# v of batch 0 in three pieces of 4, 2 and 2 heads, and a feed-forward unit moved ahead of the fourth tile, in an attention plus GEGLU kernel

## The chip, the cores and the metric

The kernel runs on one core of a Trainium2 chip. The metric is device time in microseconds (us), as the median of several executions. Executions of this kernel agree within about 0.3%. The span of a profile is up to 1.9 us shorter than the device time of the same execution, so spans are compared with spans and times with times.

Names: PE is the matmul engine, PEld its weight loads, DVE is VectorE, ACT is ScalarE, POOL is GpSimd, SP is SyncE. PSUM, the matmul results' memory, is used here as eight banks.

## The reference, cut to what matters

```python
q, k, v: (8 batches, 8 heads, 576 rows, 64)            # float32
q_p = [relu(q)*cos, relu(q)*sin];  k_p likewise          # by position
kv  = k_p^T v ;  z = sum of k_p over rows                # per batch and head
x   = (q_p kv) / (q_p z + 1e-6)  -> (4608 tokens, 512)
out = (gelu(x @ w_gate) * (x @ w_val)) @ w_out           # 512 -> 1536 -> 512
```

## The kernel before

The 576 rows of a batch are four tiles of 128 and one of 64. Tile t of batch 0 goes through these steps: scale q (`sq`), turn it (`q_by_pe`, copied out of PSUM by ScalarE or VectorE), multiply it by kv (`numer_mm`), divide (`norm`, VectorE), and turn x (`x_by_pe`, `X`). The columns of the feed-forward part that x then allows are done in units: a `gate` (four matmuls, then a Gelu on ScalarE) and a `value` (four matmuls, then a product on VectorE). `A` stands for the 256 columns of the first two tiles. `dummies(n)` are filler matmuls, whose results nobody reads. A transfer of k or v comes as two, one for the odd and one for the even partitions, and a tile needs both.

```python
def gate(n, jt, c0, w, gb):            # gb: PSUM bank
    for ct in range(CT): nc.tensor.matmul(ps[:, gb, 0:w], ...)
    nc.scalar.activation(gel[:, 0:w], ps[:, gb, 0:w], AF.Gelu)
def value(n, jt, c0, w, vb):
    for ct in range(CT): nc.tensor.matmul(ps[:, vb, 0:w], ...)
    nc.vector.tensor_mul(hT..., gel[:, 0:w], ps[:, vb, 0:w])
def gv_unit(n, jt, c0, w, gb, vb, mid=()):      # gate, mid, value
...
def Y(t, bank): ...      # numerator of tile t into banks bank and bank+1, then norm
def X(t, bank, eng): ... # turn x of tile t
...
q_by_pe(0, 3, 6, "s")                  # tile 3, copied by ScalarE
gate(0, 2, *A, 5)
X(2, 0, "v")()
sq(4, 1, "s"), sq(4, 0, "v")           # scale q of the last tile
gate(0, 3, *A, 4)
value(0, 2, *A, 7)
Y(3, 0)()
value(0, 3, *A, 2)
q_by_pe(0, 4, 3, "s")
gv_unit(0, 0, 256, 128, 5, 6)
gv_unit(0, 1, 256, 128, 4, 7, (X(3, 0, "s"),))
Y(4, 2)()
...
# k and v of batch 1: issued when the first piece of w_out has landed
nc.gpsimd.tensor_copy(kf[0:2, 0, 0, 0:1], wo_sb[0:2, 2, C - 1:C])
load_k(1)
```

Each engine is given its work in the order of the text. The tiles are counted from 0: tile 3 is the fourth. The recorded texts sometimes say "the third tile" for it.

Of the kernel before, what the change touches and what calls it, by code (L numbers as in the profile page):

```python
# [16 lines left out]
def kernel(  # L17
# [44 lines left out]
    vf = sb.tile([128, H, NJ + 1, D], FP32, name="vf")  # L62
# [13 lines left out]
    def load(dst, t, b, h0=0, h1=H, even=None, odd=None, j0=0, j1=NJ + 1):  # L76
        runs = t[b, h0:h1].rearrange("h (i r) d -> i h r d", r=9)
        for s, r0, n, eng in ((1, 5, 4, odd), (0, 0, 5, even)):
            n = min(n, j1)
            (eng or nc.sync).dma_start(  # L80
                out=dst[s:128:2, h0:h1, j0:n].rearrange("p h j d -> p h (j d)"),
                in_=runs[:, :, r0 + j0:r0 + n].rearrange("i h r d -> i h (r d)"),
            )
# [14 lines left out]
    nc.gpsimd.memset(vf[:, :, NJ], 0.0)  # L98
    load(qf, q, 0, j1=2)
    load(vf, v, 0, 0, 4)  # L100
    load(vf, v, 0, 4, 8)
    load(qf, q, 0, j0=2)

    nc.vector.tensor_scalar(par_i, par_i, 1, None, op0=ALU.bitwise_and)  # L104
# [20 lines left out]
    def dummies(n, bank=7):  # L125
        for _ in range(n):
            nc.tensor.matmul(ps[:, bank, :], lhsT=junk[:, 0:128], rhs=junk, start=True, stop=True)  # L127


    def scale(f, j, which, eng, h0=0, h1=H):  # L130
        dst, src = f
        col = (cos_c if which == 0 else sin_c)[:, j:j + 1]
        s, d = src[:, h0:h1, j, :], dst[:, j, h0:h1, which * D:(which + 1) * D]
        if eng == "v":
            nc.vector.tensor_scalar(d, s, col, 0.0, op0=ALU.mult, op1=ALU.max)  # L135
        else:
            nc.scalar.activation(d, s, AF.Relu, scale=col)  # L137

    def cast_v(b, h0, h1, eng="v"):
        cp = nc.vector.tensor_copy if eng == "v" else nc.scalar.copy  # L140
        cp(vx[b % 2][:, :, h0:h1, 0:D], vf[:, h0:h1].rearrange("p h j d -> p j h d"))  # L141
# [6 lines left out]
        )  # L148


    def kv_half(b, g, bank, eng="s"):
        for h in range(4 * g, 4 * g + 4):
            for j in range(NJ + 1):
                nc.tensor.matmul(  # L154
                    ps[:, bank, (h % 4) * (D + 1):(h % 4 + 1) * (D + 1)],
                    lhsT=kp[:, j, h, :],
                    rhs=vx[b % 2][:, j, h, 0:D + 1],
                    start=(j == 0), stop=(j == NJ),
                )
        if eng is not None:  # L160
            kv_evac(b, g, bank, eng)

    def kv_evac(b, g, bank, eng):
        src = ps[:, bank, 0:4 * (D + 1)].rearrange("p (h e) -> p h e", e=D + 1)
        dst = kv[b % 2][:, 4 * g:4 * g + 4, 0:D + 1]
        (nc.scalar.copy if eng == "s" else nc.vector.tensor_copy)(dst, src)
# [10 lines left out]
    def norm(xb, bank, g0, g1, rows=128):  # L177

        n = g1 - g0
        nd = ps[0:rows, bank + g0:bank + g1, 0:4 * (D + 1)].rearrange("p g (h e) -> p g h e", e=D + 1)  # L180
        den = rot.tile([128, 2, 4], FP32, name="den")
        nc.vector.tensor_scalar(den[0:rows, 0:n], nd[:, :, :, D], EPS, None, op0=ALU.add)  # L182
        rec = rot.tile([128, 2, 4], FP32, name="rec")
        nc.vector.reciprocal(rec[0:rows, 0:n], den[0:rows, 0:n])  # L184
        nc.vector.tensor_tensor(  # L185
            xb[0:rows, g0:g1], nd[:, :, :, 0:D],
            rec[0:rows, 0:n, :, None].to_broadcast([rows, n, 4, D]), op=ALU.mult,
        )

    def new_xb():  # L190
        return rot.tile([128, 2, 4, D], BF16, name="xb", bufs=4)
# [22 lines left out]
    def gate(n, jt, c0, w, gb):  # L214

        p0 = starts[n] + c0
        for ct in range(CT):
            nc.tensor.matmul(  # L218
                ps[:, gb, 0:w], lhsT=wg_sb[:, ct, jt * 128:(jt + 1) * 128],
                rhs=xT[:, ct, p0:p0 + w], start=(ct == 0), stop=(ct == CT - 1),  # L220
            )
        gels[n, jt, c0] = gel = rot.tile([128, 512], FP32, name="gel", bufs=4)
        nc.scalar.activation(gel[:, 0:w], ps[:, gb, 0:w], AF.Gelu)  # L223

    def value(n, jt, c0, w, vb):

        p0 = starts[n] + c0
        for ct in range(CT):
            nc.tensor.matmul(  # L229
                ps[:, vb, 0:w], lhsT=wv_sb[:, ct, jt * 128:(jt + 1) * 128],  # L230
                rhs=xT[:, ct, p0:p0 + w], start=(ct == 0), stop=(ct == CT - 1),
            )
        gel = gels.pop((n, jt, c0))
        nc.vector.tensor_mul(hT[n % 2][:, jt, 64 + c0:64 + c0 + w], gel[:, 0:w], ps[:, vb, 0:w])  # L234

    def gv_unit(n, jt, c0, w, gb, vb, mid=()):
        gate(n, jt, c0, w, gb)
        for f in mid:
            f()
        value(n, jt, c0, w, vb)  # L240
# [63 lines left out]
    def load_w(j0, j1):  # L304
        nc.gpsimd.dma_start(out=wg_sb[:, :, j0 * 128:j1 * 128], in_=wg_r[:, :, j0 * 128:j1 * 128])
        nc.gpsimd.dma_start(out=wv_sb[:, :, j0 * 128:j1 * 128], in_=wv_r[:, :, j0 * 128:j1 * 128])
# [13 lines left out]
    def q_by_pe(b, j, bank, eng, h0=0, h1=H):  # L320

        qb = ps[:, bank, :].bitcast(BF16).rearrange("p (h t) -> p h t", h=H)
        for h in range(h0, h1):
            nc.tensor.transpose(out=qb[:, h, :], in_=qp[:, j, h, :], identity=ident)  # L324
        if eng is not None:
            q_evac(b, j, bank, eng, h0, h1)

    def q_evac(b, j, bank, eng, h0=0, h1=H):
        qb = ps[:, bank, :].bitcast(BF16).rearrange("p (h t) -> p h t", h=H)
        cp = nc.vector.tensor_copy if eng == "v" else nc.scalar.copy  # L330
        if j < NJ:
            cp(qT[b % 2][:, j, h0:h1], qb[:, h0:h1])
        else:
            cp(qT[b % 2][:, j, h0:h1, 0:64], qb[:, h0:h1, 0:128:2])

    def x_by_pe(b, t, xb, bank, eng, c0=0, c1=CT):
        p0 = b * S + t * 128
        cp = nc.vector.tensor_copy if eng == "v" else nc.scalar.copy
        xb2 = xb.rearrange("p g h d -> p (g h d)")
        rows = 128 if t < NJ else 64  # L340
        view = ps[:, bank, 0:256].bitcast(BF16).rearrange("p (c t) -> p c t", c=CT)
        for ct in range(c0, c1):
            nc.tensor.transpose(  # L343
                out=view[:, ct, 0:rows], in_=xb2[0:rows, ct * 128:(ct + 1) * 128], identity=ident[0:rows, 0:rows],
            )
        cp(xT[:, c0:c1, p0:p0 + rows], view[:, c0:c1, 0:rows])  # L346

    def sq(j, which, eng, *h):
        scale(Q, j, which, eng, *h)
# [11 lines left out]
    load_w(0, 2)  # L361
    load_w(2, 4)
    load_w(4, 8)
    for j in range(2):
        sq(j, 0, "v"), sq(j, 1, "s")
        q_by_pe(0, j, j, None)
    dummies(3)
    q_evac(0, 0, 0, "v")
    cast_v(0, 0, 2, "v")
    cast_v(0, 2, 4, "s")  # L370
    kv_half(0, 0, 4, None)
    q_evac(0, 1, 1, "v")
    dummies(2)
    cast_v(0, 4, 6, "v")
    cast_v(0, 6, 8, "s")
    kv_evac(0, 0, 4, "v")
    kv_half(0, 1, 5, "s")
    x0, x1 = new_xb(), new_xb()
    numer_mm(0, 0, 6, 0)
    norm(x0, 6, 0, 1)  # L380
    dummies(1, 4)
    numer_mm(0, 0, 6, 1)
    sq(2, 1, "s")
    norm(x0, 6, 1, 2)
    sq(2, 0, "v")
    numer_mm(0, 1, 0, 0)
    numer_mm(0, 1, 0, 1)
    norm(x1, 0, 0, 2)
    x_by_pe(0, 0, x0, 4, "s", 0, 2)
    dummies(2, 5)  # L390
    x_by_pe(0, 0, x0, 4, "s", 2, 4)
    q_by_pe(0, 2, 3, None)

    nc.gpsimd.tensor_copy(tiny[0:1, 1:2], x0[0:1, 1, 3, D - 1:D])
    load_w(8, 12)
# [2 lines left out]
    A, Bw = (0, 256), (256, 320)  # L398
    xs = {1: x1}

    def X(t, bank, eng):
        return lambda: x_by_pe(0, t, xs[t], bank, eng)

    def Y(t, bank):
        def f():
            xs[t] = numer(0, t, bank, 128 if t < NJ else 64)
        return f

    gate(0, 0, 0, 128, 5)
    gate(0, 1, 0, 128, 4)  # L410
    X(1, 2, "s")()
    q_evac(0, 2, 3, "v")
    sq(3, 0, "v"), sq(3, 1, "s")
# [5 lines left out]
    value(0, 0, 128, 128, 2)  # L419
    value(0, 1, 128, 128, 3)  # L420
    q_by_pe(0, 3, 6, "s")
    gate(0, 2, *A, 5)
    X(2, 0, "v")()
    sq(4, 1, "s"), sq(4, 0, "v")
    gate(0, 3, *A, 4)
    value(0, 2, *A, 7)
    Y(3, 0)()
    value(0, 3, *A, 2)
    q_by_pe(0, 4, 3, "s")
    gv_unit(0, 0, 256, 128, 5, 6)  # L430
    gv_unit(0, 1, 256, 128, 4, 7, (X(3, 0, "s"),))
    Y(4, 2)()
    gv_unit(0, 0, 384, 128, 5, 1)
    gv_unit(0, 1, 384, 128, 4, 0)
    gate(0, 4, *A, 5)
    X(4, 7, "v")()
    gate(0, 5, *A, 4)
    gv_unit(0, 2, *Bw, 2, 6)
    gv_unit(0, 3, *Bw, 3, 7)
    value(0, 4, *A, 1)  # L440
    value(0, 5, *A, 2)
    gv_unit(0, 0, 512, 64, 4, 6)
    gv_unit(0, 1, 512, 64, 5, 7)


    load_q(1, nc.gpsimd)
# [24 lines left out]
    for jt in range(4, 12):  # L471
        for i, (c0, w) in enumerate((A, Bw)):
            if (jt, i) not in ((4, 0), (5, 0)):
                j = 0 if jt == 4 else i
# [57 lines left out]
    for n in range(1, 7):  # L532
        b = n + 1
# [5 lines left out]
        s = 0 if n > 1 else -1  # L539
# [70 lines left out]
```

## Time and profile before

| | before |
|---|---|
| device time, median | 326.25 us (325.94 to 326.5, 4 runs; 326.3 over the first 3) |
| span of the profile | 324.7 us |
| PE busy | 317.4 us (98%) |
| PE idle between 20 and 26 us | 0.08 us |
| product of batch 1's k and v begins | 48.68 us |

The page and chain of waits of this kernel are in the prediction below. PE has almost nothing left to give, so a change of the first 30 us shows as the lateness or earliness with which PE leaves that stretch.

### The profile page before, as it was taken

Reading aid. Unit: us, or ns where it says so; the run is one execution under the profiler, and the core shown is the slowest. Engines: PE = TensorE matmul, PEld = TensorE weight load, DVE = VectorE, ACT = ScalarE, POOL = GpSimd, SP = SyncE. Lnnn points to the kernel's source line nnn. Section 1 sums busy time; section 2 is a strip of 40 time slices with the busy share of each in tenths; the row PEclk is TensorE's granted clock in tenths of the full one; section 3 lists DMA queues with packets and bytes.
Section 4 is the critical chain, followed back from the end, with each engine's and each line's share of the span. In section 5 each row is a group of like instructions: output and inputs, shape, how many; then the busy total and the mean of one; then the engine's idle time right before and its main releaser. Section 6 shows DMA issues by size and latency. Waiting matters only on the chain.

```text
span 324.7 us, 5863 instructions
## 1 busy us (share of the span) xinstructions
PE 317.4 (98%) x2218; PEld 167.3 (52%) x2218; DVE 168.2 (52%) x380; ACT 151.3 (47%) x271; POOL 22.0 (7%) x43
## 2 busy tenths in 40 slices
PE   7999999999999999999999999999999999999994
PEld 2597856455445544544455445544554444444443
DVE  5785776677663575366636574637454222222210
ACT  6574774852583247325642565237522222323321
POOL 2650010000100010001000100010000100100000
PEclk9999999999999999999999999999999999999999
DMA  7999999999999929991999279946433111000124
GB/s 228 284 204 275 232 295 311 333 217 155 299 193 356 206 50 194 324 245 51 191 324 239 55 147 299 302 66 121 107 70 78 32 32 34 32 32 32 37 63 97
DMA packets 88299, 55.56 MB, mean 171 GB/s; under 512 B 53072, under 2 KB 83536, under 8 KB 88272
## 3 DMA queue, kind: packets, MB, share of 16 engines
q1 hardware_dynamic: 81744, 48.84, 60.8%
q0 software_dynamic: 6096, 5.90, 10.2%
q10 hardware_dynamic: 432, 0.46, 0.5%
q8 instruction: 17, 0.28, 0.4%
q14 instruction: 10, 0.08, 0.1%
HBM read 37.75 MB, written 9.44 MB: 145 GB/s over the span
## 4 chain that ended last, share of the span: by engine, by line
PE 94%; DVE 3%; issue 1%; ACT 0%; DVEq 0%
PE ps L218 28%; PE ps L229 28%; PE ps L259 27%; PE ps L154 3%; PE ps L170 3%; PE ps L127 3%; DVE kp L135 1%; PE ps L324 1%; PE ps L277 1%; DVE vx L141 1%; PE ps L343 1%; DVE xb L185 0%; DVE rec L184 0%; ACT xT L346 0%; DVE qp L135 0%
## 5 line engine op out<-in xcount | busy, mean ns | idle before, releaser
L234 DVE TENSOR_TENSOR hT<-gel,ps 128x512 bf16<-128x512 f32 (+5 forms) x126 | 76.2, 608 | 92.1 <-PE ps L229 91.7
L218 PE MATMUL ps<-xT,wg_sb 128*128 128x512 bf16 (+5 forms) x504 | 113.4, 349 | 0.1
L229 PE MATMUL ps<-xT,wv_sb 128*128 128x512 bf16 (+5 forms) x504 | 113.2, 348 | 0.0
L223 ACT ACTIVATE gel<-ps 128x512 f32<-128x512 f32 (+5 forms) x126 | 67.4, 536 | 73.9 <-PE ps L218 48.8
L259 PE MATMUL ps<-wo_sb,hT 128*128 128x512 bf16 x420 | 96.5, 379 | 0.0
L218 PEld LDWEIGHTS <-wg_sb 128*128 128x128 bf16 x504 | 47.1, 98 | 44.5
L229 PEld LDWEIGHTS <-wv_sb 128*128 128x128 bf16 x504 | 45.7, 98 | 39.0
L259 PEld LDWEIGHTS <-hT 128*128 128x128 bf16 x420 | 40.8, 98 | 47.7
L288 ACT COPY o_sb<-ps 128x512 f32<-128x512 f32 x35 | 20.5, 586 | 76.0 <-PE ps L259 75.9
L185 DVE TENSOR_TENSOR xb<-ps,rec 128x512 bf16<-128x512 f32 (+2 forms) x41 | 27.8, 678 | 1.8 <-DMA xr<-xb 0.3
L182 DVE TENSOR_SCALAR den<-ps 128x8 f32<-128x8 f32 (+2 forms) x41 | 6.7, 164 | 41.1 <-PE ps L170 41.0
L137 ACT ACTIVATE kp<-kf,sin_c 128x512 bf16<-128x512 f32 (+1 forms) x41 | 25.4, 681 | 0.3 <-DMA kf<-in_k_dram 0.3
L170 PEld LDWEIGHTS <-qT 128*128 128x128 bf16 (+1 forms) x320 | 15.1, 98 | 8.3 <-issue 0.4
L137 ACT ACTIVATE qp<-qf,sin_c 128x512 bf16<-128x512 f32 x28 | 19.3, 714 | 0.0
L135 DVE TENSOR_SCALAR kp<-kf,cos_c 128x512 bf16<-128x512 f32 (+1 forms) x45 | 18.7, 463 | 0.8 <-DMA kf<-in_k_dram 0.8
L135 DVE TENSOR_SCALAR qp<-qf,cos_c 128x512 bf16<-128x512 f32 x40 | 17.8, 488 | 0.0
L170 PE MATMUL ps<-kv,qT 128*128 128x65 bf16 (+1 forms) x320 | 16.6, 194 | 0.1
L209 POOL COPY xT<-xr 128x256 bf16<-128x256 bf16 x7 | 2.8, 401 | 198.0 <-DMA xr<-xb 198.0
L127 PE MATMUL ps<-hT 128*128 128x512 bf16 x34 | 11.1, 484 | 1.7 <-DVE par_i L104 1.7
L154 PEld LDWEIGHTS <-kp 128*128 128x128 bf16 x320 | 10.8, 97 | 3.2 <-issue 0.9
L154 PE MATMUL ps<-vx,kp 128*128 128x65 bf16 x320 | 11.1, 193 | 0.6 <-DVE vx L141 0.3
L141 ACT CAST vx<-vf 128x1280 bf16<-128x1280 f32 (+1 forms) x9 | 9.7, 1076 | 1.2 <-DMA vf<-in_v_dram 1.2
(54 smaller groups left out, 89.0 us busy)
## 6 DMA issues: line engine op xcount, KB each, us to landing
out_dram<-o_sb SPq DMA_DIRECT2D x38, 128.0 KB, 2.4
kf<-in_k_dram SPq DMA_DIRECT2D x7, 640.0 KB, 7.1
out_dram<-o_sb SPq DMA_DIRECT2D x16, 256.0 KB, 2.8
qf<-in_q_dram SPq DMA_DIRECT2D x6, 640.0 KB, 5.9
vf<-in_v_dram SPq DMA_DIRECT2D x6, 640.0 KB, 8.8
kf<-in_k_dram SPq DMA_DIRECT2D x7, 512.0 KB, 6.0
qf<-in_q_dram SPq DMA_DIRECT2D x6, 512.0 KB, 4.9
vf<-in_v_dram SPq DMA_DIRECT2D x6, 512.0 KB, 7.8
```

The source lines that it names most:

```text
L127: nc.tensor.matmul(ps[:, bank, :], lhsT=junk[:, 0:128], rhs=junk, start=True, stop=True)
L135: nc.vector.tensor_scalar(d, s, col, 0.0, op0=ALU.mult, op1=ALU.max)
L137: nc.scalar.activation(d, s, AF.Relu, scale=col)
L154: nc.tensor.matmul(ps[:, bank, (h % 4) * (D + 1):(h % 4 + 1) * (D + 1)], lhsT=kp[:, j, h, :], rhs=vx[b % 2][:, j, h, 0:D + 1], start=(j == ...
L170: nc.tensor.matmul(ps[0:rows, bank + g, (h % 4) * (D + 1):(h % 4 + 1) * (D + 1)], lhsT=qT[b % 2][:, t, h, 0:rows], rhs=kv[b % 2][:, h, 0:D ...
L185: nc.vector.tensor_tensor(xb[0:rows, g0:g1], nd[:, :, :, 0:D], rec[0:rows, 0:n, :, None].to_broadcast([rows, n, 4, D]), op=ALU.mult,)
L218: nc.tensor.matmul(ps[:, gb, 0:w], lhsT=wg_sb[:, ct, jt * 128:(jt + 1) * 128], rhs=xT[:, ct, p0:p0 + w], start=(ct == 0), stop=(ct == CT - 1),
L223: nc.scalar.activation(gel[:, 0:w], ps[:, gb, 0:w], AF.Gelu)
L229: nc.tensor.matmul(ps[:, vb, 0:w], lhsT=wv_sb[:, ct, jt * 128:(jt + 1) * 128], rhs=xT[:, ct, p0:p0 + w], start=(ct == 0), stop=(ct == CT - 1),
L234: nc.vector.tensor_mul(hT[n % 2][:, jt, 64 + c0:64 + c0 + w], gel[:, 0:w], ps[:, vb, 0:w])
L259: nc.tensor.matmul(ps[:, bank, :], lhsT=hT[n % 2][:, jt, c0:c0 + 128], rhs=wo_sb[:, jt, :], start=(jt == 0), stop=(jt == JT - 1),)
L288: nc.scalar.copy(o_sb, ps[:, bank, :])
```

## The change

It has two halves. The **start**: the second half of v is loaded in two transfers and multiplied by two heads at a time, the second query tile is copied in halves by ScalarE, and four filler matmuls go. It is meant to bring the first x, and so the first gate, forward. The **order after the first gate**: tile 2 of q is turned after the first two gates, x of tile 2 is turned before the gates of columns 2 and 3, and one unit, `gv_unit(0,0,256)`, moves up ahead of the fourth tile's numerator, to give PE work whose weights are there while later weights land. PSUM banks are renumbered to fit. The core of the diff:

```diff
-    load(vf, v, 0, 4, 8)
+    load(vf, v, 0, 4, 6)
+    load(vf, v, 0, 6, 8)
...
-    dummies(3)
-    q_evac(0, 0, 0, "v")
+    dummies(2)
     cast_v(0, 0, 2, "v")
     cast_v(0, 2, 4, "s")
-    kv_half(0, 0, 4, None)
-    q_evac(0, 1, 1, "v")
-    dummies(2)
+    kv_heads(0, 0, 4, 4)
+    q_evac(0, 0, 0, "v")
+    q_evac(0, 1, 1, "s", 0, 4)
     cast_v(0, 4, 6, "v")
-    cast_v(0, 6, 8, "s")
-    kv_evac(0, 0, 4, "v")
-    kv_half(0, 1, 5, "s")
+    cast_v(0, 6, 7, "v")
+    kv_evac(0, 0, 4, "s")
+    cast_v(0, 7, 8, "s")
+    dummies(1)
+    kv_heads(0, 4, 6, 5)
...                                        (kv_heads(0, 6, 8, 5) later; q scalings moved to VectorE)
-    q_by_pe(0, 2, 3, None)
     gate(0, 0, 0, 128, 5)
     gate(0, 1, 0, 128, 4)
+    q_by_pe(0, 2, 3, None)
...
     q_by_pe(0, 3, 6, "s")
+    X(2, 0, "v")()
     gate(0, 2, *A, 5)
-    X(2, 0, "v")()
+    gate(0, 3, *A, 4)
     sq(4, 1, "s"), sq(4, 0, "v")
-    gate(0, 3, *A, 4)
+    gv_unit(0, 0, 256, 128, 1, 2)
+    Y(3, 0)()
     value(0, 2, *A, 7)
-    Y(3, 0)()
-    value(0, 3, *A, 2)
-    q_by_pe(0, 4, 3, "s")
-    gv_unit(0, 0, 256, 128, 5, 6)
-    gv_unit(0, 1, 256, 128, 4, 7, (X(3, 0, "s"),))
-    Y(4, 2)()
+    value(0, 3, *A, 3)
+    q_by_pe(0, 4, 6, "s")
+    gv_unit(0, 1, 256, 128, 5, 2, (X(3, 0, "s"),))
+    Y(4, 3)()
...                                        (the next units only change banks)
```

More of the change, by code (lines that the diff above doesn't have):

```diff
@@ L148, in turn_q, with kv_heads @@
         )
-    def kv_half(b, g, bank, eng="s"):
-        for h in range(4 * g, 4 * g + 4):
+    def kv_heads(b, h0, h1, bank):
+        for h in range(h0, h1):
             for j in range(NJ + 1):
@@ L159, in kv_half @@
                 )
-        if eng is not None:
-            kv_evac(b, g, bank, eng)
+    def kv_half(b, g, bank, eng="s"):
+        kv_heads(b, 4 * g, 4 * g + 4, bank)
+        kv_evac(b, g, bank, eng)
     def kv_evac(b, g, bank, eng):
@@ L363 @@
     load_w(4, 8)
-    for j in range(2):
-        sq(j, 0, "v"), sq(j, 1, "s")
-        q_by_pe(0, j, j, None)
-    dummies(3)
-    q_evac(0, 0, 0, "v")
+    sq(0, 0, "v"), sq(1, 1, "s"), sq(0, 1, "v"), sq(1, 0, "v")
+    q_by_pe(0, 0, 0, None)
+    q_by_pe(0, 1, 1, None)
+    dummies(2)
     cast_v(0, 0, 2, "v")
     cast_v(0, 2, 4, "s")
-    kv_half(0, 0, 4, None)
-    q_evac(0, 1, 1, "v")
-    dummies(2)
+    kv_heads(0, 0, 4, 4)
+    q_evac(0, 0, 0, "v")
+    q_evac(0, 1, 1, "s", 0, 4)
     cast_v(0, 4, 6, "v")
-    cast_v(0, 6, 8, "s")
-    kv_evac(0, 0, 4, "v")
-    kv_half(0, 1, 5, "s")
+    cast_v(0, 6, 7, "v")
[3 more added lines that the diff above has]
+    kv_heads(0, 4, 6, 5)
     x0, x1 = new_xb(), new_xb()
@@ L380 @@
     norm(x0, 6, 0, 1)
-    dummies(1, 4)
+    kv_heads(0, 6, 8, 5)
+    kv_evac(0, 1, 5, "s")
+    q_evac(0, 1, 1, "s", 4, 8)
+    dummies(1, 3)
     numer_mm(0, 0, 6, 1)
-    sq(2, 1, "s")
     norm(x0, 6, 1, 2)
-    sq(2, 0, "v")
+    x_by_pe(0, 0, x0, 4, "s", 0, 2)
+    sq(2, 0, "v"), sq(2, 1, "v")
     numer_mm(0, 1, 0, 0)
@@ L388 @@
     norm(x1, 0, 0, 2)
-    x_by_pe(0, 0, x0, 4, "s", 0, 2)
-    dummies(2, 5)
     x_by_pe(0, 0, x0, 4, "s", 2, 4)
-    q_by_pe(0, 2, 3, None)
     nc.gpsimd.tensor_copy(tiny[0:1, 1:2], x0[0:1, 1, 3, D - 1:D])
@@ L421 @@
     q_by_pe(0, 3, 6, "s")
+    X(2, 0, "v")()
     gate(0, 2, *A, 5)
-    X(2, 0, "v")()
+    gate(0, 3, *A, 4)
     sq(4, 1, "s"), sq(4, 0, "v")
-    gate(0, 3, *A, 4)
+    gv_unit(0, 0, 256, 128, 1, 2)
+    Y(3, 0)()
     value(0, 2, *A, 7)
-    Y(3, 0)()
-    value(0, 3, *A, 2)
-    q_by_pe(0, 4, 3, "s")
-    gv_unit(0, 0, 256, 128, 5, 6)
-    gv_unit(0, 1, 256, 128, 4, 7, (X(3, 0, "s"),))
-    Y(4, 2)()
+    value(0, 3, *A, 3)
+    q_by_pe(0, 4, 6, "s")
+    gv_unit(0, 1, 256, 128, 5, 2, (X(3, 0, "s"),))
+    Y(4, 3)()
     gv_unit(0, 0, 384, 128, 5, 1)
-    gv_unit(0, 1, 384, 128, 4, 0)
+    gv_unit(0, 1, 384, 128, 6, 2)
     gate(0, 4, *A, 5)
     X(4, 7, "v")()
-    gate(0, 5, *A, 4)
-    gv_unit(0, 2, *Bw, 2, 6)
-    gv_unit(0, 3, *Bw, 3, 7)
-    value(0, 4, *A, 1)
-    value(0, 5, *A, 2)
-    gv_unit(0, 0, 512, 64, 4, 6)
-    gv_unit(0, 1, 512, 64, 5, 7)
+    gate(0, 5, *A, 0)
+    gv_unit(0, 2, *Bw, 1, 6)
+    gv_unit(0, 3, *Bw, 2, 7)
+    value(0, 4, *A, 3)
+    value(0, 5, *A, 4)
+    gv_unit(0, 0, 512, 64, 5, 6)
+    gv_unit(0, 1, 512, 64, 1, 7)
     load_q(1, nc.gpsimd)
```

## The prediction

> **What bounds the kernel now.** I read the page first, then the chain of waits in order of time, then the timeline around its gaps, then the landing times of single transfers and the stretch table of DMA share. The page says that the matmul engine hardly rests:
>
> ```profile
> PE 317.4 (98%) x2218; PEld 167.3 (52%) x2218; DVE 168.2 (52%) x380; ACT 151.3 (47%) x271; POOL 22.0 (7%) x43
> DMA  7999999999999929991999279946433111000124
> ```
>
> The reader is to see two things: PE is busy for 98% of the span, so only 7 us of it are idle at all; and the DMA row, in slices of 324.7/40 = 8.1 us, stays at 9 for 13 slices after the first, far beyond the stretch that the change edits. The diff touches only work up to about 30 us; from block 1 on both kernels are the same text. So the question is what an earlier finish of the start-up is worth at the next place where PE waits. The chain of waits shows the places:
>
> ```profile
> 15.64 0.49 DVE qp L135
> 16.13 0.05 issue
> 16.17 0.62 PE ps L324 x8
> ...
> 23.36 0.03 issue
> 23.39 0.59 ACT xT L346
> ...
> 44.72 0.09 DVE hT L234
> 44.81 0.31 issue
> 45.13 1.08 DVE kp L135 x2
> 46.20 0.29 issue
> 46.49 1.27 DVE kp L135 x3
> 47.76 0.88 DVE vx L141
> 48.64 0.04 issue
> 48.68 1.36 PE ps L154 x40
> ```
>
> Until 16.17 the chain hops between engines; after it PE runs without a break but for 0.66 us at 23.36 (the third tile's x) and, above all, **the passage at 44.7 to 48.7**, where the chain leaves PE for k and v of batch 1. After 48.68 it stays on PE. The timeline of that passage:
>
> ```profile
> 44.70 2.56 ACT L137 ACTIVATE kp<-kf,sin_c 128x512 bf16<-128x512 f32 x4 [0.16 <-DMA kf<-in_k_dram]
> 45.13 2.63 DVE L135 TENSOR_SCALAR kp<-kf,cos_c 128x512 bf16<-128x512 f32 x5
> 47.24 0.59 ACT L288 COPY o_sb<-ps 128x512 f32<-128x512 f32 x1
> 47.73 0.72 ACT L137 ACTIVATE kp<-kf,sin_c 128x512 bf16<-128x512 f32 x1
> 48.68 1.36 PE L154 MATMUL ps<-vx,kp 128*128 128x65 bf16 x40 [0.18 <-DVE vx L141]
> ```
>
> The first line is the one that decides: ScalarE's sine half of k **already waits for the k transfer** (0.16 us), although the chain blames DVE. From there ScalarE is full: 44.70 + 2.56, then the 0.59 copy, then the fifth k piece, which ends at 47.73 + 0.72 = 48.45. The k-v product needs that piece, so it can't begin before about 48.5 as long as k lands when it does.
>
> When does k land? Its even half:
>
> ```profile
> kf<-in_k_dram SPq DMA_DIRECT2D x1, 640.0 KB, 8.1
> ```
>
> It is issued at about 36.45 and lands at 44.55. Its issue hangs on the first piece of w_out (issued at 22.69, 12.7 us to landing, so 35.4; the GpSimd marker copy runs at 35.47 and the k issue at 35.78). And that piece stands behind the gate and value weights. The stretch table gives a DMA share between 0.99 and 2.04 in every microsecond from 3 to 47, so this stream is never empty: its end is set by bytes, not by when PE is ready.
>
> **What the Trainium skill says.** "DMA: Bandwidth & Descriptors", section "Issuing engines are not separate DMA queues": transfers started by different engines run on the same 16 DMA engines and interleave. The trace agrees: the queues of SyncE and GpSimd together hold that share. "Perfetto Trace Analysis", section "DMA Optimizations", says that splitting transfers may help if the DMA engines are generally idle; here they aren't, so the split of v can only let its first part land earlier within the same stream. "TensorE: Matmul & The Clock Gate", Part 1: PE runs at half rate until it has been busy for a window of about 3.4 us, and a window of idleness brings half rate back. The trace agrees with the first half: weight loads of the warm-up matmuls come 0.43 us apart up to 7.69 and then 11 in 2.28 us. The gaps that four fewer filler matmuls can open are about half a microsecond, far below a window, so I expect no slow clock. "Perfetto Trace Analysis", section "Identifying the Most-Contended Engine", warns that matmul busy time overstates PE; weight loads at 52% say so too, but here I use only the order of work.
>
> **The change part by part.** Every duration is from a row of the timeline of before.
> - Filler matmuls: 8 become 4; two took 0.43 us in the chain, so 4 x 0.215 = 0.86 us of PE work goes, in a stretch where PE otherwise waits.
> - v in six transfers, not four: four issues took 2.62 us, so two more put the second q transfer 1.3 us later (6.90 to 8.2). It landed at 14.15; I expect 14.2 to 15. Its first use moves to about 15.0, so most of that is hidden. Same bytes, same row sizes.
> - First four heads: before, DVE copied the first query tile (0.61 us) ahead of its v cast, and the product began at 12.16. Now the casts come first: v landed at 10.4, cast 0.55 on DVE and 0.72 on ScalarE, so 11.2; PE is held by transposes and two fillers to 11.6. The product begins at 11.6, **0.5 us earlier**.
> - Its copy goes from DVE behind casts (13.08) to ScalarE (12.4 to 12.8), so the first numerator starts at about 12.8 instead of 13.82. The x of the first half then ends near 13.9 (before 14.98).
> - Second half: v lands at 12.1 in either kernel; casts of one head each on DVE and ScalarE, and products by 2 heads, end near 13.4; copy 13.9; numerator, three DVE steps (0.16 + 0.2 + 0.42 less overlap), so x of tile 0 at 15.0 instead of 15.7. The first gate, which started at 16.63, starts at 15.7; the gate weights (issued 9.32, 6.0 us) land at 15.3, so **0.9 us earlier**, and this is close to the weights' own limit.
> - Given back: the second tile's normalization now waits behind two q scalings on DVE (2 x 0.44), so x of tile 1 is ready near 16.9, and the transposes of tile 2 (0.45), formerly ahead of the gates, now lie after them. At the first value matmuls the lead is 0.4 (17.2 for 17.6).
> - Tile 3: the units of w columns 2 to 4 need transfers that landed at 19.2 (10.94 + 8.3) and 20.4 (11.66 + 8.7); before, their gate ran at 19.62 and their value at 20.72, so they had only 0.4 and 0.3 in hand. The new order puts a unit with early weights (0.44 of PE) between them and so keeps the lead at about 0.5. The third tile's gap of 0.66 shrinks to about 0.3.
> Sum at the start of the output matmuls (44.45): PE arrives **0.5 to 0.9 us earlier**, about 0.7.
>
> What this is worth: DVE's k work starts not at 45.13 but at the landing, 44.65, so it ends 0.48 earlier; ScalarE's starts at 44.70 as before and ends at 48.45. The product moves from 48.68 to about 48.5. So the lead of 0.7 us becomes **about 0.2 us**, and the other 0.5 becomes a longer wait of PE ahead of that product. 326.3 - 0.2 = 326.1.
>
> **The rivals.**
> - The lead goes through in full (k lands earlier too): 325.6. For it: the w_out and q issues on GpSimd hang on start-up work (ScalarE's last q scaling) and would go out a little sooner. Against: value weights issued at 16.85 land only at 30.5, so that queue has a long backlog when these issues join it.
> - The start-up gets slower: the later q transfer, one more scaling on DVE or the late weights hold the gates. Then the 0.18 of slack is used up and the rest counts in full: 326.4 to 326.9. For it: DVE is full from 14 to 17 us; the weights have 0.3 us in hand. Against: the lead of 0.9 at the first gate comes before these.
> - Nothing moves, since transfers alone set the passage: 326.3. For it: three runs of before spread over 0.56 us, more than my 0.2.
> - The different assignment of transfers to semaphores (two more on SyncE) delays transposes later on. Against: after 62 us no wait of PE above 0.5 us in total is left, and those transfers have long waits ahead of their use.
>
> **Range and chances.** Middle 326.1; from full lead less noise, 325.4, to a lost start-up, 326.8. 2% is 6.5 us, which is as much as all idle time of PE in the span; neither way do I see it: faster 0.005, same 0.985, slower 0.01.
>
> **What would show it.** Right: the first v product near 11.6, the first gate near 15.7, the output matmuls start near 43.8, the w_out marker stays near 35.5 and k's even half lands at 44.3 to 44.9, ScalarE waits for k for more than 0.16 us (about 0.8), and PE's wait before the batch 1 product grows from 0.18 to about 0.7. From there both traces run parallel, 0.2 apart. Wrong: the k transfer lands over 0.3 us earlier or later; a PE gap over 0.5 us between 16 and 24; or a different distance between that product and the end.

## More of the kernel before

From the timeline of the kernel before (start, duration, engine, source line, operation, out<-in, count):

```profile
18.75 0.45 ACT L223 ACTIVATE gel<-ps 128x128 f32<-128x128 f32 x2
...
19.82 1.01 ACT L332 COPY qT<-ps 128x1024 bf16<-128x1024 bf16 x1 [0.62 <-PE ps L324]
...
20.73 0.39 ACT L223 ACTIVATE gel<-ps 128x256 f32<-128x256 f32 x1
21.00 0.72 ACT L137 ACTIVATE qp<-qf,sin_c 128x512 bf16<-128x512 f32 x1
21.15 0.42 PE L170 MATMUL ps<-kv,qT 128*128 128x65 bf16 x8
...
24.02 0.38 PE L218 MATMUL ps<-xT,wg_sb 128*128 128x128 bf16 x4
...
24.50 0.67 ACT L223 ACTIVATE gel<-ps 128x128 f32<-128x128 f32 x2 [0.53 <-PE ps L218]
```

ScalarE copies the fourth tile's q, does one Gelu, and scales q of the last tile. Meanwhile PE's numerator of the fourth tile runs as one group of eight matmuls at 21.15, with no wait in brackets: the copy that it needs is done at 20.83, and none of the other ScalarE instructions stands in its way. The first and last lines are Gelus that serve as marks further down. The stretch table of 20 to 26 us, whose first columns are the stretch, its length and PE's busy time with the number of matmuls:

```profile
20.00:26.00 6.00, 5.92 (x89) 5.30 (x88) 4.77 (x15) 4.42 (x11) 3.14 (x4) 1.00 1.24 208
```

So PE is idle for 6.00 - 5.92 = 0.08 us here, all of it just before the gate at 24.02.

## The result, and the profile after

The changed kernel takes **327.8 us** (327.54 to 328.16, 4 runs) against 326.25 us: ratio 1.0049, interval 1.0031 to 1.0066. The change is within 2%, as predicted, but the time lies outside the predicted range of 325.4 to 326.8. It lost about 1.5 us where a gain of 0.2 was expected.

The page of the changed kernel, the two lines that answer to those of before:

```profile
PE 314.7 (96%) x2181; PEld 166.8 (51%) x2214; DVE 168.5 (52%) x381; ACT 150.9 (46%) x272; POOL 22.4 (7%) x43
...
DMA  7999999998999929991999379986433111000124
```

PE is busy 2.7 us less in a longer span. Not all of that is idleness: PEld lost only four loads, those of the fillers, while PE lost 37 matmuls, so most of these are missing records. The DMA row is nearly as before.

**Where the time goes.** Both kernels run the same Gelus, so comparing the start of the same Gelu in the two timelines gives PE's lateness over the whole run. At the first Gelu (17.05 us in before) the changed kernel is 0.50 us early, at the third (18.75) 0.11 us late. At the ninth (24.5 us in before) it is **1.24 us late**, and the lateness stays at 1.24 us to the last Gelu, at 309 us. So the loss is made in less than 6 us. The stretch table of the changed kernel for that time:

```profile
20.00:26.00 6.00, 5.10 (x78) 4.63 (x76) 4.09 (x14) 3.77 (x9) 3.13 (x4) 1.00 1.24 206
```

PE's idle time there is 6.00 - 5.10 = 0.90 us, where it was 0.08. And its timeline shows where (the first and last lines are the two marks):

```profile
18.86 0.45 ACT L226 ACTIVATE gel<-ps 128x128 f32<-128x128 f32 x2
...
21.35 0.29 PE L173 MATMUL ps<-kv,qT 128*128 128x65 bf16 x4
...
22.00 0.28 ACT L226 ACTIVATE gel<-ps 128x128 f32<-128x128 f32 x1
22.31 0.29 DVE L237 TENSOR_TENSOR hT<-gel,ps 128x128 bf16<-128x128 f32 x1 [1.25 <-ACT gel L226]
22.33 0.29 PE L173 MATMUL ps<-kv,qT 128*128 128x65 bf16 x4 [0.68 <-ACT gel L226]
22.33 0.16 PEld L173 LDWEIGHTS <-qT 128*128 128x128 bf16 x3 [0.78 <-issue]
...
24.61 0.33 PEld L173 LDWEIGHTS <-qT 128*64 128x64 bf16 x8 [0.18 <-ACT qT L337]
...
25.27 0.21 PEld L221 LDWEIGHTS <-wg_sb 128*128 128x128 bf16 x3 [0.19 <-issue]
...
25.75 0.66 ACT L226 ACTIVATE gel<-ps 128x128 f32<-128x128 f32 x2 [0.53 <-PE ps L221]
```

The numerator of the fourth tile is torn in two: four matmuls at 21.35, the other four at 22.33, and the bracket says that PE waited for a Gelu. Two smaller waits follow, for ScalarE's copies of q and x. Idle times of the weight loads, 0.78 + 0.18 + 0.19 = 1.15 us, are close to the growth from 0.11 to 1.24. ("Perfetto Trace Analysis" of the Trainium skill, section "Tensor Engine Instruction (MATMUL, LD_WEIGHTS)", says that the matmuls' end times are a model; that fits the same hole reading 0.68 on the matmul row and 0.78 on the weight row.) The chain of waits of the changed kernel says why that Gelu was late (start, length, what):

```profile
19.93 0.76 ACT qT L335
...
20.84 0.30 ACT gel L226
21.13 0.26 issue
21.39 0.72 ACT qp L138
22.11 0.18 ACT gel L226
22.29 0.04 issue
22.33 0.30 PE ps L173 x4
```

The chain, which was on PE here before, now lies on ScalarE for over 2 us. Read it upward from the last line: PE's second half waits for the Gelu of the moved unit; that Gelu stands behind the scaling of q's last tile, two other Gelus and the copy of q's fourth tile. ScalarE takes them in order. The same page and section calls ScalarE's queue strictly first in, first out, and this chain agrees, with 0.72 us for the scaling alone. Why should a numerator wait for a Gelu at all? The moved unit's gate has bank 1, and `Y(3, 0)` writes its second half to bank 1.

The passage of batch 1's k, from the changed kernel's timeline:

```profile
45.69 2.55 ACT L138 ACTIVATE kp<-kf,sin_c 128x512 bf16<-128x512 f32 x4
...
49.92 1.36 PE L155 MATMUL ps<-vx,kp 128*128 128x65 bf16 x40 [0.18 <-DVE vx L142]
```

The even half of k lands at 44.98 (44.60 before), but ScalarE comes to it only at 45.69 and has no wait in brackets any more. The product begins at 49.92 instead of 48.68, again 1.24 us late.

### The profile page after: what moved, and what is told of

It reads as the page before. It is cut to its first block, busy times and chain, and to the rows that moved or that the text cites. A ratio compares the mean times of both kernels' runs of the same rounds, so it can differ in the third digit from the quotient of the medians.

```text
span 326.3 us, 5822 instructions
## 1 busy us (share of the span) xinstructions
PE 314.7 (96%) x2181; PEld 166.8 (51%) x2214; DVE 168.5 (52%) x381; ACT 150.9 (46%) x272; POOL 22.4 (7%) x43
## 4 chain that ended last, share of the span: by engine, by line
PE 90%; DVE 4%; DMA 2%; issue 1%; ACT 1%; POOL 0%; DVEq 0%; POOLq 0%; ACTq 0%
PE ps L232 28%; PE ps L221 28%; PE ps L262 26%; PE ps L155 3%; PE ps L173 3%; DMA kf<-in_k_dram 2%; DVE kp L136 2%; PE ps L280 1%; PE ps L327 1%; DVE xb L188 1%; DVE vx L142 1%; DVE qp L136 1%; PE ps L346 0%; DVE hT L237 0%; DVE rec L187 0%
## 5 line engine op out<-in xcount | busy, mean ns | idle before, releaser
L221 PE MATMUL ps<-xT,wg_sb 128*128 128x512 bf16 (+5 forms) x491 | 111.6, 348 | 1.2 <-ACT xT L349 0.5
L232 PE MATMUL ps<-xT,wv_sb 128*128 128x512 bf16 (+5 forms) x497 | 111.8, 348 | 0.4
L262 PE MATMUL ps<-wo_sb,hT 128*128 128x512 bf16 x408 | 94.1, 379 | 0.6
L138 ACT ACTIVATE qp<-qf,sin_c 128x512 bf16<-128x512 f32 x26 | 17.9, 713 | 0.0
L136 DVE TENSOR_SCALAR qp<-qf,cos_c 128x512 bf16<-128x512 f32 x40 | 17.6, 479 | 0.0
L128 PE MATMUL ps<-hT 128*128 128x512 bf16 x29 | 9.1, 476 | 1.7 <-DVE par_i L105 1.7
L142 ACT CAST vx<-vf 128x1280 bf16<-128x1280 f32 (+2 forms) x9 | 9.4, 1047 | 0.9 <-DMA vf<-in_v_dram 0.9
```

The costliest lines, as they stand in the source:

```text
L136: nc.vector.tensor_scalar(d, s, col, 0.0, op0=ALU.mult, op1=ALU.max)
L138: nc.scalar.activation(d, s, AF.Relu, scale=col)
L142: cp(vx[b % 2][:, :, h0:h1, 0:D], vf[:, h0:h1].rearrange("p h j d -> p j h d"))
L221: nc.tensor.matmul(ps[:, gb, 0:w], lhsT=wg_sb[:, ct, jt * 128:(jt + 1) * 128], rhs=xT[:, ct, p0:p0 + w], start=(ct == 0), stop=(ct == CT - 1),
L232: nc.tensor.matmul(ps[:, vb, 0:w], lhsT=wv_sb[:, ct, jt * 128:(jt + 1) * 128], rhs=xT[:, ct, p0:p0 + w], start=(ct == 0), stop=(ct == CT - 1),
L262: nc.tensor.matmul(ps[:, bank, :], lhsT=hT[n % 2][:, jt, c0:c0 + 128], rhs=wo_sb[:, jt, :], start=(jt == 0), stop=(jt == JT - 1),)
```

## The experiments

Theory: the moved unit causes the loss, since its Gelu stands late in ScalarE's order and PE and VectorE both need it. Rivals: the divided v and its delayed transfers; the new start as a whole; the turning of q's tile 2 behind the gates; or k of batch 1 landing later.

### Which half of the change

`head_only` keeps the new start and takes back the order; `tail_only` does the reverse.

```diff
 # head_only, against after: everything from the first gate on as in before, and
+    q_by_pe(0, 2, 3, None)          # ahead of the gates again
 # tail_only, against before: only
-    q_by_pe(0, 2, 3, None)          # ahead of the gates
...                                  # and the whole order after the first gate as in after
```

> The changed start (v in three pieces, copies in halves, fewer fillers) with the old order of work from the first gate on, and the second q tile's transposes back ahead of the gates. Theory 1 (the loss is the PE hole near 21.5 us, where the third tile's numerator waits for a PSUM bank that a Gelu has not read yet): the start costs nothing, so 326.0 to 326.5 against 326.3 of before. Theory 2 (the loss is in the start: k lands at 7.7 instead of 6.9 because of the divided v, and all follows later): 326.8 to 327.6, and k lands late again.

Measured: 326.10 us, ratio 0.9988 (0.9975 to 1.0).

> The old start with the new order of work from the first gate on. Theory 1: the hole of about 0.8 us is here, with two followers of 0.2 to 0.4, so 327.2 to 327.8. Theory 2: no more than 326.6, and k lands near 6.9 as before.

Measured: 327.75 us, ratio 1.0037 (1.0024 to 1.0049). Its lateness goes from -0.08 us to +1.24 us over the same 6 us. The loss belongs to the order after the first gate. The start is not slower.

### Is it the divided v?

`v_halves` is the changed kernel with v's second half in one transfer pair.

```diff
-    load(vf, v, 0, 4, 6)
-    load(vf, v, 0, 6, 8)
+    load(vf, v, 0, 4, 8)
```

> The changed kernel with v loaded in two halves of four heads, as before; everything else as changed. Theory 2: k lands at 6.9 again and 0.5 to 0.8 us comes back: 327.0 to 327.3. Theory 1 and 3: no gain, 327.7 to 328.1 (the second half's first cast may start a little later).

Measured: 327.84 us, ratio 1.0038 (1.0025 to 1.0051), lateness 0.19 growing to 1.32. The growth, 1.13 us, is that of the changed kernel, so undividing v takes nothing of the hole away. (The ratio is 1.0049 for the changed kernel, taken in another session; the two intervals overlap.)

### The bank, and ScalarE's order

`bank6` gives the moved unit's gate another bank; `sq4_late` puts the q scaling on ScalarE behind the unit's Gelu; `bank6_sq4` does both.

```diff
 # bank6
-    gv_unit(0, 0, 256, 128, 1, 2)
+    gv_unit(0, 0, 256, 128, 6, 2)
 # sq4_late
-    sq(4, 1, "s"), sq(4, 0, "v")
+    sq(4, 0, "v")
     gv_unit(0, 0, 256, 128, 1, 2)
+    sq(4, 1, "s")
```

> The changed kernel, with the gate of the third tile's first unit put into PSUM bank 6 instead of 1, so that the numerator's second half has bank 1 free. Theory 1: the hole goes and 0.6 to 1.0 us comes back: 326.8 to 327.2 against 327.8. Theory 3 (the bank only shows the lateness of ScalarE, on which a 1.0 us copy and a q scaling stand ahead of that Gelu, and the third tile's x hangs on that Gelu through VectorE's order anyway): the hole moves to the third tile's transposes, and at most 0.3 comes back: 327.5 to 327.8. Theory 2: 327.8.

Measured: 327.27 us, ratio 1.0025 (1.0011 to 1.0038); lateness 0.02 growing to 0.65. Its timeline:

```profile
22.22 0.29 DVE L237 TENSOR_TENSOR hT<-gel,ps 128x128 bf16<-128x128 f32 x1 [1.26 <-PE ps L232]
...
23.61 0.40 PE L346 MATMUL ps<-ident,xb 128*128 128x128 bf16 x4 [0.30 <-DVE xb L188]
```

The numerator is whole again, but the unit's product on VectorE still waits 1.26 us: its matmuls are the releaser that the profile names, but they end at 21.51, and the unit's Gelu at 22.19. So it is the Gelu that VectorE waits for. The division of the fourth tile is next in VectorE's order, so PE waits 0.30 us for that x.

> The changed kernel with one thing moved: the sine scaling of the fifth q tile on ScalarE (0.72 us) goes behind the Gelu of the third tile's first unit instead of ahead of it; bank 1 stays. Theory 3 (ScalarE's order sets the hole): that Gelu ends near 21.7 instead of 22.3, the hole of PE shrinks by 0.6, and 0.4 to 0.7 us comes back: 327.1 to 327.4 against 327.8. Theory 1 (the bank alone): the same size, since the bank is free earlier too. Theory 4 (neither; the loss comes from the later copies for tiles 3 and 4): 327.7 or more.

Measured: 327.22 us, ratio 1.0023 (1.001 to 1.0035); lateness -0.20 growing to +0.34. Its timeline:

```profile
21.04 0.67 PE L173 MATMUL ps<-kv,qT 128*128 128x65 bf16 x8
...
24.36 0.38 PE L221 MATMUL ps<-xT,wg_sb 128*128 128x128 bf16 x4 [0.21 <-ACT xT L349]
```

One group again, stretched to 0.67 us, and the later wait for x is still there.

> Both the free bank and the later scaling. Theories 1 and 3 together: the hole is gone, and the third tile's x no longer waits for the late Gelu, so 0.9 to 1.2 us come back in all: 326.5 to 326.9. If either alone was the whole cause, no more than in its own run (327.3).

Measured: 327.48 us (327.05 to 327.66), ratio 1.0029 (1.0016 to 1.0042). Its profile, taken in its fastest execution, shows lateness growing from -0.29 to +0.08, thus by 0.37; but the time is no better than with one edit alone, a miss against the expected 326.5 to 326.9. The growth was 1.13 us in the changed kernel. One edit takes 0.50 of it, the other 0.59, both 0.76: not their sum, since they act on the same hole. Part of what the time lost beyond the lateness is taken up below; why the median lies 0.4 us above the profiled execution is not known.

`tail_fixed` is `tail_only` with both edits.

> The old start with the new order of work from the first gate on, with both the free bank and the later q scaling. If the loss of the new order is those two waits, it is as fast as the kernel before: 326.3 to 326.8. If the order has more against it (the fourth tile's copies on ScalarE stand behind the fifth q tile's), 326.9 to 327.3.

Measured: 327.12 us, ratio 1.0016 (1.0003 to 1.0028); lateness 0.16 growing to 0.65. Without the new start, too, the two edits give back part: 0.6 of the 1.2 us in time, and 0.83 of the 1.32 us by which the lateness of `tail_only` grew.

### The moved unit itself

`unit_back` is the changed kernel with only the unit back in its old place, behind q's last tile.

```diff
-    gv_unit(0, 0, 256, 128, 1, 2)
     Y(3, 0)()
     value(0, 2, *A, 7)
     value(0, 3, *A, 3)
     q_by_pe(0, 4, 6, "s")
-    gv_unit(0, 1, 256, 128, 5, 2, (X(3, 0, "s"),))
+    gv_unit(0, 0, 256, 128, 4, 2)
+    gv_unit(0, 1, 256, 128, 5, 7, (X(3, 0, "s"),))
```

> The changed kernel with only the third tile's first unit (gate and value, 0.44 us of PE work) put back behind the fifth q tile's transposes, as before the change. Theory U (moving that unit is the whole loss: it stands where its Gelu is late, and it is missing where ScalarE copies the fifth q tile and the fourth x tile): 326.1 to 326.6, the kernel before or a little better. Theory V (0.5 us of the loss has another source, such as the two gates ahead of the values or the second tile's x ahead of them): 326.8 to 327.2.

Measured: 326.57 us (326.02 to 326.91), ratio 0.9997 (0.9984 to 1.0009). The numerator in its timeline, then its stretch table:

```profile
21.09 0.43 PE L173 MATMUL ps<-kv,qT 128*128 128x65 bf16 x8
```

```profile
20.00:26.00 6.00, 5.92 (x88) 5.07 (x86) 4.86 (x16) 4.25 (x11) 3.18 (x5) 1.00 1.24 206
```

The numerator is whole, PE's idle time between 20 and 26 us is back at 0.08 us, and the time is that of before. **The moved unit makes the hole, and most of the loss.** Its share of the growth is 1.13 - 0.22 = 0.91 us. It is not the whole loss: the kernel with the same start and the old order took 325.99 us in the same session (`head_again`, below), 0.6 less by the medians and 0.4 by the means. The intervals of the two ratios overlap, but the traces point the same way (at the last Gelu `unit_back` is 0.42 us late and `head_again` 0.18 early), so the rest of the new order seems to cost about 0.4 us. Half of that can be seen in the trace of `unit_back`: the numerator's weight loads wait 0.21 us for ScalarE's copy of the fourth tile's q, since the numerator now comes before both value groups and not after the first.

With bank and ScalarE's order both mended the moved unit still cost 0.37 to 0.49 us of growth against 0.22 here. This difference I read as its absence later: before, it filled PE while ScalarE copied q and x, and with it gone the 0.2 us wait for x (0.08 in the kernels that do not move it) appears in every kernel that moves it except `bank6`, where the wait for x lies ahead. That reading is argued from the traces and has no run of its own.

### Does q's tile 2 behind the gates matter, and does the start repeat?

`q2_late` is `head_only` with `q_by_pe(0, 2, 3, None)` behind the first two gates; `head_again` is `head_only` once more, in a later session.

> The best kernel so far (changed start, old order) with only the third q tile's transposes behind the first two gates, as the change has them. Theory U: no more than 0.2 us slower than that kernel, 326.0 to 326.4. Theory V': it is a source of the loss, 326.5 to 326.9.

Measured: 326.08 us, ratio 0.9983 (0.9969 to 0.9997). The rival falls: no cost in time. In its profile, though, the lead at 18.75 us is 0.02, where `head_only` has 0.25 and `head_again` 0.18.

> The changed start with the old order once more on another chip, for its gain over the kernel before: 0.3 to 0.5 us again if it is real, 326.0 to 326.2 against 326.5; 0 to 0.1 if it was chance.

Measured: 325.99 us, ratio 0.9984 (0.9972 to 0.9997). The record has both runs of this kernel on chip 10, so the session is another and the chip is not. The new start alone is the best version apart from `q2_late`, which equals it: both beat the two kernels, by a small but repeated 0.12 to 0.17%. Where that comes from is taken up below.

### What lateness and earliness are worth at the passage of batch 1

`late1` is the kernel before with five filler matmuls ahead of the first gate. `lead1` cuts the value matmuls of the last columns of block 0 from four to two (0.98 us of PE work less; the result is wrong, relative error 0.109).

```diff
 # late1
+    dummies(5)
     gate(0, 0, 0, 128, 5)
 # lead1, in value()
+        last = 2 if n == 0 and jt >= 10 else CT
-        for ct in range(CT):
+        for ct in range(last):
```

> The kernel before with five filler matmuls (5 x 0.215 = 1.08 us) ahead of the first gate: a delay of PE by 1.1 us and nothing else. Theory P (a late PE passes through in full, less the 0.2 us of slack at the k and v passage of batch 1): 327.1 to 327.5 against 326.4. Theory A (that passage waits for the transfer and absorbs it): under 326.8.

Measured: 327.64 us, ratio 1.0034 (1.0022 to 1.0047). Its timeline at ScalarE's k work:

```profile
45.83 2.54 ACT L137 ACTIVATE kp<-kf,sin_c 128x512 bf16<-128x512 f32 x4
```

No wait for k. The lateness is 1.38 us at 18.75 us, at 43 us and at the end: the passage takes nothing of it. (The five fillers made more lateness than the 1.08 us that I had reckoned, so the time lies a little above the expected range.)

> The kernel before with half of the contraction left out of the value matmuls of the last two column tiles of block 0 (a wrong result on purpose): 8 matmuls and 0.98 us of PE work less just ahead of 44 us, and nothing else. Theory P (k lands when the stream of transfers lets it, so ScalarE starts its k work at 44.7 as before): no more than 0.1 to 0.4 us comes out, 326.0 to 326.3 against 326.4, and PE's wait before the batch 1 product grows by about 0.8. Theory F (the passage follows PE): all of it, 325.4.

Measured: 326.07 us, ratio 0.9988 (0.9974 to 1.0001). Its timeline:

```profile
44.80 2.56 ACT L137 ACTIVATE kp<-kf,sin_c 128x512 bf16<-128x512 f32 x4 [1.08 <-DMA kf<-in_k_dram]
...
48.51 1.26 PE L154 MATMUL ps<-vx,kp 128*128 128x65 bf16 x36 [0.32 <-ACT kp L137]
```

PE is ahead by 0.61 us at 43 us, by 0.83 at 44 us, and by only 0.27 after the passage (0.12 of it is there from the start, before the cut, and so is spread between profiles): ScalarE waits 1.08 us for k, and the bulk of the product (36 of its 40 matmuls) begins at 48.51. So the passage is one-sided: lateness passes whole, and a lead is cut to what k's landing allows. Small leads do pass: `head_only` keeps its 0.25 us and `head_again` its 0.18, in whose profile k lands early, at 44.26.

`lead1_k` releases k and v of batch 1 earlier, by another marker, on top of `lead1`.

```diff
-    nc.gpsimd.tensor_copy(kf[0:2, 0, 0, 0:1], wo_sb[0:2, 2, C - 1:C])
+    nc.gpsimd.tensor_copy(kf[0:2, 0, 0, 0:1], wv_sb[0:2, 3, J - 1:J])
```

> The kernel with 0.98 us of PE work left out ahead of 44 us (wrong result on purpose), and with the k and v transfers of batch 1 released by the last value weights (which land at 30.5) instead of the first piece of w_out (35.4). Theory P (the transfer of k cut the lead to 0.4 before): k lands several us earlier and the whole 1.0 us comes out, 325.3 to 325.7 against 326.5. Theory Q (something else in that passage cuts the lead): 326.0 to 326.2 as with the late release. A third possibility: w_out now lands too late for the output matmuls, which would show as a PE wait there.

Measured: 326.25 us, ratio 0.9992 (0.9978 to 1.0006), also wrong. Its timeline:

```profile
30.54 1.32 SPq L80 DMA_DIRECT2D kf<-in_k_dram  x2
...
44.78 2.56 ACT L137 ACTIVATE kp<-kf,sin_c 128x512 bf16<-128x512 f32 x4 [1.11 <-DMA kf<-in_k_dram]
```

The two k transfers are issued at 30.54 instead of 35.30, and the even half still lands at 44.67 instead of 44.70. The odd half did come earlier, at 40.36 instead of 42.87, but ScalarE needs both. w_out's last piece lands at 45.17 instead of 42.1. So an earlier issue did not bring k earlier to ScalarE. I read this as one full stream in which what k gains, w_out loses; no run changed the number of bytes.

`head_fill_k` was an attempt at a better version: `head_only`, the early marker, and a gate moved forward into the wait for x. Its edit, against `head_only`:

```diff
-    gv_unit(0, 0, 384, 128, 5, 1)
-    gv_unit(0, 1, 384, 128, 4, 0)
     gate(0, 4, *A, 5)
-    X(4, 7, "v")()
+    gv_unit(0, 0, 384, 128, 6, 1)
+    gv_unit(0, 1, 384, 128, 4, 0)
     gate(0, 5, *A, 4)
+    X(4, 7, "v")()
+    value(0, 4, *A, 1)
...                        # and the marker as in lead1_k
```

> The changed start with the old order from the first gate on, plus a gate of later columns moved into the PE wait ahead of the fourth tile, plus the early release of k and v. If all hold, the start's 0.3, the wait's 0.4 and no cut by k: 325.6 to 326.0 against 326.5, better than both kernels. If the order of work fails, as it did in the changed kernel, 326.1 to 326.5.

Measured: 326.34 us, ratio 0.9993 (0.9981 to 1.0006). A miss: no better than `head_only`. The wait that this was to fill was no wait: PE's idle time before that x is 0.08 us in `head_only`, as in before. In its own order of work PE waits 0.14 us for a Gelu at 25.48, and the lead of 0.04 becomes a lateness of 0.16.

`before2` is the text of before, once, without timing rounds, for the spread of a trace.

> The kernel before once more, for the spread of its own profile: k of batch 0 landed at 6.9 us in the one profile I have, and at 7.1 to 7.7 in those of the changed start, divided v or not. If that is chance, this profile may show it at 7.0 to 7.7 too; if the changed start delays it, again 6.9.

Measured: 326.57 us, span 324.7, lateness 0.03 us against the first profile. But ScalarE, waiting for a k transfer of batch 0, goes on at 7.29 us there and at 7.03 in the first profile of the same text. It is 7.76 in the changed kernel, and 7.95 in `late1`, whose v is undivided. So the 0.73 us by which that k came later in the changed kernel's profile is not to be charged to the divided v.

### What the lateness does not explain

The span is longer by 1.6 us in the changed kernel's profile, and the lateness is 1.24. The end of the traces gives the rest (all in us, against the kernel before; landing = last store's landing after PE's last matmul, 2.89 in before; end = span's end after that landing, 1.75 in before):

| profile | lateness at the end | landing | end | sum | span |
|---|---|---|---|---|---|
| after | +1.24 | +0.71 | -0.36 | +1.59 | +1.6 |
| tail_only | +1.24 | 0.00 | -0.23 | +1.01 | +1.0 |
| v_halves | +1.32 | 0.00 | -0.02 | +1.30 | +1.3 |
| sq4_late | +0.33 | +0.72 | -0.36 | +0.69 | +0.7 |
| bank6_sq4 | +0.08 | +0.77 | -0.36 | +0.49 | +0.5 |
| unit_back | +0.42 | -0.02 | -0.36 | +0.04 | 0.0 |
| head_only | -0.07 | 0.00 | -0.36 | -0.43 | -0.4 |

Two things follow. First, of `head_only`'s gain of about 0.4 us, 0.36 lie at the very end of the program: in the kernels with the divided v the program ends 0.34 to 0.36 us sooner after its last landing. In the traces SyncE waits there for the transfers' semaphores one after another, about 0.06 us each, and the last store's stands two places later in that order. That would be 0.12 us. The other 0.24 lie behind SyncE's last such wait, in a stretch that takes 1.05 us in before and 0.82 in after, `head_only` and `tail_only`, the last with v undivided. This is seen, not tested. What is left for the start itself, about 0.1 us (0.07 and 0.18 at the last Gelu of `head_only` and `head_again`), is not shown: `lead1` and `lead1_k` have the start of before, and are ahead of it by 0.12 and 0.17 us at 18.75 us. `unit_back` has the 0.36 us from the end as well: it is still 0.42 us late on PE and equal in time. Second, in some profiles the last store lands 0.7 us later, in the changed kernel and in `sq4_late` and `bank6_sq4` (0.4 in `bank6`). All of these have both the divided v and the moved unit, and no other kernel here shows it. The changed kernel had it in its profiled execution of 328.16 us; its two faster executions have spans of 325.7. **Why it comes stays open**; it adds to the loss in some executions and is no part of the hole at 22 us.

## Why the prediction was wrong

- **The view of the bound held, but for one gap (below).** PE is the bound, only its idle stretches count, and the passage at 44.7 to 48.7 decides what a lead is worth. `lead1` shows the predicted 48.5 (48.51).
- **Fillers, v in six transfers, the first four heads, their copy.** The first product came at 11.92 (predicted 11.6, before 12.16), the first numerator at 13.15 (12.8, before 13.82), x of tile 0 at 15.44 (15.0), the first gate at 15.69 (15.7). Signs right, with 34 to 60% of the first three gains missing; the first gate started as predicted but stopped after two matmuls and went on at 16.24, waiting 0.26 us for ScalarE's second x copy. In the profile with the late k of batch 0 this may be chance in part: over all profiles the first product comes at 11.65 to 12.36 with the old start (7 profiles, mean 11.92) and at 11.30 to 11.92 with the new (10, mean 11.59). The gain is 0.3 us and not 0.5.
- **Given back.** At the first value matmuls I had "17.2 for 17.6"; it was 17.55, against 17.45 before, so that the 17.6 was misread as well. The whole lead was gone there, not 0.4 left. That is a mis-sized term, worth about 0.3 us of lead, which the passage would mostly have cut anyway.
- **The step that failed** is this: "The new order puts a unit with early weights (0.44 of PE) between them and so keeps the lead at about 0.5. The third tile's gap of 0.66 shrinks to about 0.3." I checked the unit's weights and PE's time, and not its Gelu on ScalarE nor its bank. The gap of 0.66 that it was to shrink was not there either: PE's idle time between 20 and 26 us was 0.08 us, so filler had nothing to win in that place. The Gelu ran at 22.00, behind a copy of 1.01 us and a scaling of 0.72 us; PE's numerator needed bank 1 from it and stood for 0.68 to 0.78 us; and two waits of about 0.2 us came later. In place of a lead of 0.5, PE was 1.24 us late. `unit_back` takes the hole away, and 0.91 us of the lateness.
- **What the lead is worth.** The rule was right for a lead. I wrote that beyond 0.18 us lateness "counts in full", and `late1` shows that it does. The 0.18 of slack that was to be used up first took nothing off: 1.38 us went in and came out, and in the changed kernel 1.24. With PE late, ScalarE's wait for k, which I expected at 0.8 us, is zero.
- **The transfers.** I had w_out's marker near 35.5 and k's even half landing at 44.3 to 44.9: measured 35.90 and 44.98. So this sign of being wrong, a landing over 0.3 us off, appeared too, but without effect, since ScalarE reached k at 45.69. The expectation that k's landing is set by bytes and not by its issue agrees with `lead1_k` for the half that counts; that it is the bytes is argued.
- **No rival came true as written.** The slower start-up has the right sign, but the start is not slower (`head_only`), the loss has another reason than the ones named with it (the q transfer, a scaling on VectorE, the weights), and it is 1.5 us instead of 0.1 to 0.6. The sign of being wrong, a PE gap over 0.5 us between 16 and 24 us, is the one that appeared.

"Perfetto Trace Analysis", section "Matmuls", says that independent matmul groups should rotate through different PSUM banks, so that evacuating one overlaps the next group's matmuls. The changed kernel breaks that at bank 1, and `bank6` measures it: about 0.5 us of PE lateness. It also shows the limit of the advice here, since VectorE waited for the same Gelu on its own account.

## What to carry to other kernels

When a matmul unit is moved forward as filler, follow everything that hangs on it: at which place its evacuation stands in the other engine's order, which group next writes its bank, and which later instruction stands behind its consumer. In a kernel whose matmul engine is 98% busy such a move can lose more than it could win, since here lateness passed through to the end (1.24 and 1.38 us) while a lead of 0.83 us was cut to 0.27 where a transfer set the pace. Before filling a gap, check in the stretch table that it is idle time of the engine, and not only a place where the chain of waits leaves it. And look at what the unit was hiding in the place it leaves.

## What the Trainium skill lacked or had wrong

- "Perfetto Trace Analysis", section "Matmuls": it gives the rule of rotating banks, but not that a bank comes free only when the reader's turn in its engine's order has come. Here that made a hole of 0.68 to 0.78 us out of a Gelu that lasts 0.28 us.
- The same page does not say that one late evacuation can hold PE by two roads at once, so that mending either gives back about half: 0.50 and 0.59 us of 1.13, and 0.76 together.
- "DMA: Bandwidth & Descriptors": it does not say what an earlier issue is worth when other transfers are under way. Here, issuing k 4.76 us earlier moved the landing of its second half by 0.03 us, and of its first by 2.5 us.
- No page that I read gives the spread of one landing: a k transfer of batch 0 let ScalarE go on at 7.03 and at 7.29 us in two profiles of the same text. Batch 1's even half of k landed between 44.07 and 44.98 us over all profiles with the late marker.
- The pages price the runtime's own steps behind a kernel, but none says that the program's own end after its last landing can change with an edit at its start: 1.75 us before, 1.52 in `tail_only` and 1.39 with v divided, which is most of what the new start won.
